# Linear attention and token/channel mixing: the first eight head pairs projected in float32, their numerators formed with tokens on partitions

## The chip, the cores and the metric

One core of one Trainium2 chip runs the kernel. The metric is the device time of one launch, in microseconds, as the median of several runs. TensorE (PE) multiplies matrices, VectorE (DVE), ScalarE (ACT) and GpSimd (POOL) work elementwise, SyncE (SP) issues DMAs. PEld is the loading of PE's stationary operand.

## What is computed

Per batch and head a feature map makes 256 positive features of each 64-wide query and key, a linear attention follows, and its output goes through a token mixer and a channel mixer. Shapes: batch 8, heads 8, sequence 576, head width 64, 128 features before the sign pair, token width 256, channel width 1536.

```python
def phi(x):
    proj = np.einsum('bhsd,df->bhsf', x, w_phi)
    proj = proj - np.max(np.abs(proj), axis=-1, keepdims=True)
    return np.concatenate([np.exp(proj), np.exp(-proj)], axis=-1)
q_p, k_p = (phi(q), phi(k))
kv = np.einsum('bhsf,bhsd->bhfd', k_p, v)
z = np.sum(k_p, axis=2)
num = np.einsum('bhsf,bhfd->bhsd', q_p, kv)
den = np.einsum('bhsf,bhf->bhs', q_p, z)[..., None] + 1e-06
out = num / den
...
xt = x.transpose(0, 2, 1)
h = np.maximum(xt @ w_tok1, 0.0) @ w_tok2
u = x + h.transpose(0, 2, 1)
return u + np.maximum(u @ w_ch1, 0.0) @ w_ch2
```

## The kernel before

Heads go in pairs: 4 pairs a batch, 32 in all. Nearly all matrix products are split in two float32r parts: a value is a high part plus a low part, and `mm3` (L77) makes three products of them (high by high, high by low, low by high). The weights of the mixers arrive as 64-bit numbers, and `convert` (L116) makes each block into its two parts: ACT takes an absolute value (L131), DVE does four steps on the bits (L132 to L135), ACT writes the high part and POOL the low part. 24 blocks of the channel weights and 7 of the token weights are made so, all in the first part of the program.

A pair passes these steps:

- **Projection** (`less_max`, L191). Pairs 0 to 3 (`i < PLAIN`) multiply 64-row slices of the loaded float32 tiles, queries on partitions 0 to 63 and keys on 64 to 127, by `wp` (L216); a float32 matmul is two PE records in the trace. Later pairs are first stacked by `stack` (L178): the high part on 64 partitions by DVE, the low part on the other 64 by POOL; then one float32r matmul of 256 columns gives both products (L212), ACT copies the second one out of PSUM (L219) and DVE adds (L221). DVE takes the largest absolute value (L226). The subtraction is on DVE for keys of pairs 0 to 3, on ACT for their queries, with a negated maximum from DVE (L230, L232), and on POOL for all later pairs (L234).
- **Keys** (`keys`, `add_kv`): ACT makes the two exponentials `kp` (L278), PE sums them into `pkv` (L300), 65 columns a matmul, the last column being the sum z. `kv` is copied out with z spread over 64 columns (L311), for later pairs as a high and a low part (L313).
- **Queries** (`queries`, `turn`, `numerators`): PE turns the projections so that features lie on partitions (L356), ACT makes `qf`, two signs (L363); for later pairs DVE and POOL split it into `qh` and `ql`. PE multiplies `kv` as stationary operand by `qf` (L389, pairs 0 to 3) or by the parts (L81, `pn<-qh`, `pn<-ql`): the result `pn` has channels on partitions, 320 or 256 tokens wide, and the spread z gives the denominator in the other half of the partitions. ACT copies the numerators, ACT (pairs 0 to 7, `EARLY`) or DVE adds the epsilon, DVE takes the reciprocal of the whole [128, 320] or [128, 256] tile (L401), POOL multiplies.

`token_mix` (L417) turns the attention output back to tokens on partitions with PE transposes (L423, `px`), splits it on ACT and DVE (`xh`, `xl`) and multiplies; `channel_mix` works on 18 tiles of 256 tokens (`h`, `acc`). Four streams of work and the conversion of the weights are woven together by `weave` with shares and step costs written in the code, and the build's scheduler then sets the order of every engine. PE, DVE, ACT and POOL each take their instructions in that order. The PSUM tag `rest` has three banks, which `pt`, `pn` and others share.

## Time and profile before

| | us |
|---|---|
| median of 3 runs | 1182.57 |
| lowest, highest | 1180.76, 1182.67 |
| span of the profiled execution | 1183.6 |
| PE busy | 1137.6 |
| DVE busy | 867.1 |
| POOL busy | 587.1 |
| ACT busy | 531.5 |

The profile is of one execution. Busy PE time is a poor measure here, since matmuls overlap in the pipeline: a matmul of 256 columns shows a duration of 0.28 us, while such matmuls start 0.12 us apart. The number of PE records in a stretch tells more. The clock column gives the share of TensorE's full clock that was granted: 1.00 is the higher of its two levels (2.4 GHz), 0.5 the lower (1.2 GHz); before the first change on record, some 30 us into the span, it tells nothing.

### The profile page before, as it was taken

What the parts mean: (1) busy time and instruction counts of PE and PEld (TensorE: products, weight loads), DVE (VectorE), ACT (ScalarE), POOL (GpSimd) and SP (SyncE); (2) the same over time, 40 slices, a digit from 0 to 9 for tenths busy, and PEclk for the clock granted to TensorE, in tenths of its full rate; (3) what the DMA queues carried; (4) which work ended last, traced back from release to release, by engine and by line L of the source; (5) the groups of instructions that cost most, each with busy time, mean ns of one, the idle gap of its engine ahead of it and who ended that gap; (6) DMA issues with size and microseconds to landing.
All of it is one profiled execution on the core that took longest, in us unless ns stands there. A gap on an engine that the chain in (4) does not pass through costs nothing.

```text
span 1183.6 us, 24087 instructions
## 1 busy us (share of the span) xinstructions
PE 1137.6 (96%) x9032; PEld 1102.0 (93%) x9032; DVE 867.1 (73%) x1782; ACT 531.5 (45%) x1545; POOL 587.1 (50%) x734
## 2 busy tenths in 40 slices
PE   8789897899999999999999999999999999999998
PEld 7667887898999999999999999999999999999998
DVE  7977899986777888887878677684787978763111
ACT  5767565453444445444444443343353544431110
POOL 3344775854555566465555455473564655431000
PEclk9679898999999999999999999999999999999999
DMA  9541222111111111111111011110111110000000
GB/s 232 150 135 28 72 84 71 50 31 28 31 40 32 49 31 32 49 32 49 32 34 46 20 31 49 30 50 1 49 31 49 32 48 12 19 1 19 19 19 19
DMA packets 65300, 54.31 MB, mean 46 GB/s; under 512 B 44768, under 2 KB 56416, under 8 KB 65184
## 3 DMA queue, kind: packets, MB, share of 16 engines
q1 hardware_dynamic: 63824, 52.41, 15.4%
q8 instruction: 72, 1.18, 0.4%
q10 hardware_dynamic: 1360, 0.36, 0.2%
q14 instruction: 44, 0.36, 0.1%
HBM read 43.32 MB, written 9.44 MB: 45 GB/s over the span
## 4 chain that ended last, share of the span: by engine, by line
PE 78%; DVE 11%; ACT 4%; issue 3%; POOL 2%; DMA 2%; SPq 0%; DVEq 0%; POOLq 0%; ACTq 0%
PE h L81 23%; PE acc L81 23%; PE pkv L300 8%; PE pn L81 7%; PE ph L81 3%; PE pa L81 3%; PE pt L356 3%; PE ppq L212 2%; PE ppk L212 2%; DVE qh L74 2%; PE pn L389 1%; DVE den L401 1%; PE px L423 1%; DMA rawc<-in_wc 1%; DVE bitsc L132 1%
## 5 line engine op out<-in xcount | busy, mean ns | idle before, releaser
L81 PE MATMUL acc<-gh,wc 128*128 128x256 f32 x1728 | 345.1, 283 | 0.0
L81 PEld LDWEIGHTS acc<-gh,wc 128*128 128x128 f32 x1728 | 276.0, 188 | 0.2 <-ACT gh L489 0.2
L81 PE MATMUL h<-uh,wc_h 128*128 128x256 f32 x864 | 246.8, 286 | 4.3 <-ACT wc_h L72 2.2
L81 PE MATMUL h<-uh,wc_l 128*128 128x256 f32 x864 | 245.9, 285 | 0.8 <-POOL wc_l L75 0.8
L81 PE MATMUL h<-ul,wc_h 128*128 128x256 f32 x864 | 243.9, 282 | 0.3 <-POOL ul L470 0.3
L81 PE MATMUL acc<-gl,wc 128*128 128x256 f32 x864 | 242.0, 282 | 0.6 <-DVE gl L490 0.6
L278 ACT ACTIVATE kp<-pmk 128x256 f32<-128x256 f32 (+1 forms) x320 | 109.2, 389 | 171.1 <-POOL pmk L234 168.1
L300 PE MATMUL pkv<-v,kp 128*128 128x65 f32 (+1 forms) x1152 | 165.7, 278 | 6.8 <-ACT kp L278 3.3
L81 PEld LDWEIGHTS h<-uh,wc_h 128*128 128x128 f32 x864 | 163.7, 190 | 5.8 <-ACT wc_h L72 2.6
L300 PEld LDWEIGHTS pkv<-v,kp 128*128 128x128 f32 x1152 | 155.9, 200 | 12.6 <-ACT kp L278 5.4
L75 POOL TENSOR_TENSOR ql<-qf,qh 128x320 fp32r<-128x320 f32 (+1 forms) x112 | 103.4, 923 | 127.7 <-DVE qh L74 110.8
L81 PEld LDWEIGHTS h<-uh,wc_l 128*128 128x128 f32 x864 | 163.4, 189 | 1.1 <-POOL wc_l L75 1.1
L81 PEld LDWEIGHTS h<-ul,wc_h 128*128 128x128 f32 x864 | 163.8, 190 | 0.5 <-POOL ul L470 0.5
L81 PEld LDWEIGHTS acc<-gl,wc 128*128 128x128 f32 x864 | 162.5, 188 | 0.7 <-DVE gl L490 0.7
L490 DVE SCALAR_TENSOR_TENSOR gl<-h,gh 128x512 fp32r<-128x512 f32 x108 | 73.5, 680 | 89.2 <-ACT gh L489 88.7
L74 DVE CAST qh<-qf 128x320 fp32r<-128x320 f32 (+1 forms) x224 | 106.5, 489 | 34.6 <-ACT qf L363 29.1
L401 DVE RECIPROCAL den<-den 128x320 f32<-128x320 f32 x64 | 124.6, 1947 | 3.2 <-ACT den L397 2.2
L363 ACT ACTIVATE qf<-pt 128x320 f32<-128x320 f32 (+1 forms) x256 | 92.6, 412 | 71.2 <-PE pt L356 68.5
L81 PE MATMUL pn<-qh,kv 128*128 128x320 f32 (+1 forms) x448 | 118.8, 302 | 3.5 <-DVE qh L74 1.5
L489 ACT ACTIVATE gh<-h 128x512 fp32r<-128x512 f32 x108 | 64.9, 601 | 116.0 <-PE h L81 115.2
L402 POOL TENSOR_TENSOR xt<-xt,den 128x320 f32<-128x320 f32 x64 | 53.7, 839 | 114.7 <-DVE den L401 87.8
L470 POOL TENSOR_TENSOR ul<-xt,uh 128x64 fp32r<-128x64 f32 (+3 forms) x120 | 62.2, 543 | 84.2 <-ACT uh L469 83.3
(110 smaller groups left out, 2415.3 us busy)
## 6 DMA issues: line engine op xcount, KB each, us to landing
raw<-in_qk SPq DMA_DIRECT2D x27, 576.0 KB, 3.7
rawc<-in_wc SPq DMA_DIRECT2D x24, 512.0 KB, 4.2
v<-in_vm SPq DMA_DIRECT2D x31, 256.0 KB, 3.3
out_x<-xt SPq DMA_DIRECT2D x12, 256.0 KB, 2.2
out_x<-xt SPq DMA_DIRECT2D x16, 192.0 KB, 2.0
raw<-in_w SPq DMA_DIRECT2D x8, 256.0 KB, 4.6
...
```

The source lines that it names most:

```text
L74: eng_hi.tensor_copy(hi, raw)
L75: eng_lo.tensor_tensor(lo, raw, hi.bitcast(F32), op=ALU.subtract)
L81: nc.tensor.matmul(o, a, m, start=first and i == 0, stop=last and i == 2, skip_group_check=group_ok)
L212: nc.tensor.matmul(ps[:, i].rearrange("p two f -> p (two f)"), t[:, c:c + P], wp2.rearrange("p two f -> p (two f)"), start=True, stop=True)
L278: nc.scalar.activation(kp[:, :len(us), sg], pm[:, :len(us)], AF.Exp, scale=1.0 - 2.0 * sg)
L300: nc.tensor.matmul(o, kp[:, n, sg], v, start=g == 0 and n == 0 and sg == 0, stop=u is None, skip_group_check=True)
L363: nc.scalar.activation(full, src, AF.Exp, scale=1.0 - 2.0 * sg)
L401: nc.vector.reciprocal(den, den)
L402: nc.gpsimd.tensor_tensor(x, x, den, op=ALU.mult)
L470: nc.gpsimd.tensor_tensor(l[:, d:d + n], t[:, c, o:o + n], h[:, d:d + n].bitcast(F32), op=ALU.subtract)
L489: nc.scalar.activation(gh, ph, AF.Relu)
L490: nc.vector.scalar_tensor_tensor(gl, ph, 0.0, gh.bitcast(F32), op0=ALU.max, op1=ALU.subtract)
```

## The change

Pairs 4 to 7 join pairs 0 to 3 (`PLAIN` 4 to 8): they are loaded by four DMAs a pair instead of one block for a pair of rows, aren't stacked, and are projected by float32 matmuls of 64 rows from the loaded tiles. In all eight pairs the subtraction of the maximum is one DVE instruction for queries too; the negated maximum and ACT's part in it are gone.

The numerators of pairs 0 to 7 (`ROWS`) are formed the other way round: a block of 128 (or 64) tokens of `qf` is the stationary operand, and `kv` with its sum column, 65 columns wide, moves. The result `pr` has tokens on partitions; both heads of a piece share a bank. DVE adds the epsilon to the few denominators, takes their reciprocals and multiplies into `rows`; one piece later (`flip`) PE turns `rows` to channels (`pf`) and ACT copies it to `xt`. The token mixer of batches 0 and 1 reads `rows` itself, without `px`, and makes `xl` on POOL.

Counted in the two orders: on PE 32 float32 `pn` matmuls, 96 float32r `pn` matmuls, 72 stacked projections and 40 `px` transposes go; 160 `pr` matmuls (32 of them with 64 tokens), 72 more float32 projections and 40 `pf` transposes come. DVE has 32 instructions fewer, ACT 148, POOL 73; SP has 12 more DMAs.

```diff
-PLAIN = 4
-EARLY = 8
+PLAIN = 8
+ROWS = 8
...
-        if base == 0:
-            nmx = column(wk, 2, tag="nmx", name=f"nmx{name}")
-            nc.vector.tensor_scalar(nmx[:, :n], mx[:, :n], -1.0, None, op0=ALU.mult)
-            for i in range(n):
-                nc.scalar.activation(pm[:, i], pr[:, i], AF.Identity, bias=nmx[:, i:i + 1])
-        else:
-            eng.tensor_tensor(pm[:, :n], pr, mx[:, :n].unsqueeze(2).to_broadcast([P, n, F]), op=ALU.subtract)
+        eng.tensor_tensor(pm[:, :n], pr, mx[:, :n].unsqueeze(2).to_broadcast([P, n, F]), op=ALU.subtract)
...
+        if i < ROWS:
+            kv = wk.tile([P, 2, 4, D], F32, tag="kv0", name=f"kv0_{i}", bufs=1)
+            kv = kv.rearrange("p s j d -> p (s j d)")[:, :4 * (D + 1)]
+            nc.scalar.copy(kv, pkv.rearrange("p s j d -> p (s j d)"))
+            kvs[i] = kv.rearrange("p (s j d) -> p s j d", s=2, j=2)
+            return
...
+            if row_major:
+                flip(*row_major)
+                yield 0.2
+            row_major = None
             if split_up:
                 yield from until(lambda: split_up[0] in kvs)
-                numerators(*split_up)
+                if split_up[0] < ROWS:
+                    row_major = row_numerators(*split_up)
+                else:
+                    numerators(*split_up)
                 yield 0.75
...
+    def row_numerators(i, k, j, qps):
+        b, p = divmod(i, NP)
+        h, p = divmod(p, 2)
+        n = 3 - k
+        if j == 0:
+            sums[0] = ps_w.tile([P, 2, 3, D + 1], F32, **REST, name=f"pr{i}_{k}")
+        pn = sums[0]
+        at = (D if j == 1 else 0) if k == 0 else 0
+        for u in range(n):
+            w, c = (P, at + u * P) if u < 2 else (D, 0 if j == 1 else 2 * P)
+            for sg in range(2):
+                nc.tensor.matmul(pn[:w, j, u], qps[sg][:, c:c + w], kvs[i][:, sg, j],
+                                 start=j == 0 and u == 0 and sg == 0, stop=j == 1 and u == n - 1 and sg == 1,
+                                 skip_group_check=True)
+        if j == 0:
+            return None
...
+        den = column(wk, 8, tag="dn", name=f"dn{i}_{k}")
+        for w, a, e in ((P, 0, 2), (D, 2, 3))[:2 - k]:
+            d = den[:w, 2 * a:2 * e].rearrange("p (j u) -> p j u", j=2)
+            nc.vector.tensor_scalar(d, pn[:w, :, a:e, D], 1e-6, None, op0=ALU.add)
+            nc.vector.reciprocal(d, d)
+            nc.vector.tensor_tensor(x[:w, :, a:e], pn[:w, :, a:e, :D],
+                                    d.unsqueeze(3).to_broadcast([w, 2, e - a, D]), op=ALU.mult)
+        return i, k
+
+    def flip(i, k):
+        b, p = divmod(i, NP)
+        make_xts(b)
+        x = rows_of[b, p // 2][:, 3 * k:3 * k + 3 - k, (p % 2) * P:(p % 2) * P + P]
+        pf = ps_w.tile([P, SEG[0][1]], F32, **REST, name=f"pf{i}_{k}")[:, :SEG[k][1]]
+        for u in range(3 - k):
+            w = P if u < 2 else D
+            nc.tensor.transpose(pf[:, u * P:u * P + w], x[:w, u], ident[:w, :w])
+        nc.scalar.copy(xts[b][k][:, p], pf)
+        if k == 1:
+            attended.add(i)
...
-            px = bank(b, [P, 2, P], f"px{b}_{h}_{u}", 1)
-            for c in range(2):
-                nc.tensor.transpose(px[:w, c], xt[k][:, 2 * h + c, o:o + w], ident)
+            if (b, h) in rows_of:
+                px = rows_of[b, h][:, u].rearrange("p (c d) -> p c d", c=2)
+            else:
...
-            split(xh, xl, px[:w], nc.scalar, nc.vector)
+            split(xh, xl, px[:w], nc.scalar, nc.gpsimd if (b, h) in rows_of else nc.vector)
```

The order of three places. First PE in the numerators of pair 0 (the last number but one of a name is not the pair; each tile has its own number). Before, with `pn` multiplied by 256 tokens at a time:

```order
L356 MATMUL pt_10_383<-ident,pmq_10_354 128x128 x2
L216 MATMUL ppq_00_449<-wp,pair_299 128x128 x2
L300 MATMUL pkv_359<-v_97,kp_2_380 128x65 x4
L300 MATMUL pkv_359<-v_97,kp_3_427 128x65 x4
L216 MATMUL ppq_01_487<-wp,pair_301 128x128
L216 MATMUL ppk_1_535<-wp,pair_497 128x128
L389 MATMUL pn_10_415<-qf_100_386,kv_0_320 128x256
L389 MATMUL pn_10_415<-qf_101_388,kv_0_320 128x256
L356 MATMUL pt_11_430<-ident,pmq_11_409 128x128 x2
```

After, from the end of the second piece of `pr`:

```order
L399 MATMUL pr_0_312<-kv_0_310,qf_010_323 64x65
L399 MATMUL pr_0_312<-kv_0_310,qf_011_325 64x65
L292 MATMUL pkv_344<-v_95,kp_2_370 128x65 x4
L214 MATMUL ppq_00_440<-wp,pair_289 128x128 x2
L214 MATMUL ppk_4_455<-wp,pair_291 128x128
L214 MATMUL ppq_01_476<-wp,pair_291 128x128 x2
L214 MATMUL ppk_0_492<-wp,pair_483 128x128 x2
L292 MATMUL pkv_344<-v_95,kp_3_420 128x65 x4
L423 MATMUL pf_0_403<-ident,rows_0_355 128x128 x2
L399 MATMUL pr_1_408<-kv_0_310,qf_100_376 128x65
```

The transposes `pf` stand 8 matmuls of the keys' sums and 7 projections behind the `pr` matmuls that they depend on, and the next `pr` stands behind them; before, nothing on PE at this place waits for a normalised numerator.

DVE at the same place, before, around the reciprocal of pair 0's first denominators:

```order
L132 TENSOR_SCALAR bitsc_1_1130<-bitsc_1_1130 128x512
L135 SCALAR_TENSOR_TENSOR bitsc_3_0_714<-rawc_3_0_712,bitsc_3_0_714 128x512
L134 SCALAR_TENSOR_TENSOR bitsc_0_870<-rawc_0_868,bitsc_0_870 128x512
L133 TENSOR_SCALAR bitsc_1_1130<-bitsc_1_1130 128x512
L401 RECIPROCAL den_0_325<-den_0_325 128x320
L226 TENSOR_REDUCE mxq_00_452<-ppq_00_449 128x2
L135 SCALAR_TENSOR_TENSOR bitsc_0_870<-rawc_0_868,bitsc_0_870 128x512
```

After, between the epsilon and the product of pair 0's first rows (`dn_0_356` is the denominators' tile, `rows_0_355` what `pf` turns):

```order
L133 SCALAR_TENSOR_TENSOR bitsc_2_0_537<-rawc_2_0_535,bitsc_2_0_537 128x512
L130 TENSOR_SCALAR bitsc_0_850<-bitsc_0_850 128x512
L226 TENSOR_TENSOR pmk_3_418<-ppk_3_413,mxk_3_416 128x256
L132 SCALAR_TENSOR_TENSOR bitsc_3_0_699<-rawc_3_0_697,bitsc_3_0_699 128x512
L411 RECIPROCAL dn_0_356<-dn_0_356 128x4
L224 TENSOR_REDUCE mxq_00_443<-ppq_00_440 128x2
L224 TENSOR_REDUCE mxk_4_457<-ppk_4_455 128x1
L131 TENSOR_SCALAR bitsc_0_850<-bitsc_0_850 128x512
L224 TENSOR_REDUCE mxq_01_479<-ppq_01_476 128x2
L130 TENSOR_SCALAR bitsc_1_1076<-bitsc_1_1076 128x512
L133 SCALAR_TENSOR_TENSOR bitsc_3_0_699<-rawc_3_0_697,bitsc_3_0_699 128x512
L412 TENSOR_TENSOR rows_0_355<-pr_0_312,dn_0_356 128x2x2x64
```

The one long reciprocal has become a reciprocal of 4 columns and a product; six conversion steps of the weights (`bitsc`) stand between the epsilon, which is the row ahead of these, and the product.

Second, DVE in the second batch. Before, queries of pair 4, the last keys of pair 5 and the stacking of the next pairs:

```order
L186 CAST stk_1660<-raw_1652 64x640
L75 TENSOR_TENSOR ql_010_1384<-qf_010_1381,qh_010_1383 128x320
L186 CAST stq_1680<-raw_1652 64x640
L221 TENSOR_TENSOR pq_11_1519<-ppq_11_1514,partq_11_1517 128x256
L221 TENSOR_TENSOR pk_4_1557<-ppk_4_1553,partk_4_1555 128x128
L74 CAST qh_100_1496<-qf_100_1494 128x256
L226 TENSOR_REDUCE mxq_11_1521<-pq_11_1519 128x2
L226 TENSOR_REDUCE mxk_4_1559<-pk_4_1557 128x1
L75 TENSOR_TENSOR ql_100_1497<-qf_100_1494,qh_100_1496 128x256
L449 SCALAR_TENSOR_TENSOR al_1_1420<-pa_1_1242,ah_1_1419 128x512
L74 CAST qh_101_1502<-qf_101_1500 128x256
L401 RECIPROCAL den_0_1327<-den_0_1327 128x320
```

After, where the same token mixer as in the rows before (the first batch's second half, `al_1`, `ph_1`) has come as far; `rows_0_1283` is of pair 4:

```order
L224 TENSOR_REDUCE mxk_4_1417<-ppk_4_1415 128x1
L226 TENSOR_TENSOR pmk_4_1419<-ppk_4_1415,mxk_4_1417 128x128
L410 TENSOR_SCALAR dn_0_1284<-pr_0_1203 128x4
L411 RECIPROCAL dn_0_1284<-dn_0_1284 128x4
L412 TENSOR_TENSOR rows_0_1283<-pr_0_1203,dn_0_1284 128x2x2x64
L410 TENSOR_SCALAR dn_0_1284<-pr_0_1203 64x2
L411 RECIPROCAL dn_0_1284<-dn_0_1284 64x2
L506 TENSOR_TENSOR xt_0_401<-ph_1_0_0_1338,xt_0_401 128x320
L412 TENSOR_TENSOR rows_0_1283<-pr_0_1203,dn_0_1284 64x128
L224 TENSOR_REDUCE mxk_0_1496<-ppk_0_1493 128x2
L224 TENSOR_REDUCE mxq_11_1349<-ppq_11_1346 128x2
```

The casts and differences of `qf`, the stacking and the long reciprocal are gone; denominators and rows stand there, and projections are read from PSUM directly.

Third, SP at the start. Before:

```order
L253 DMA pair_102<-in_qk 64x512
L253 DMA pair_104<-in_qk 64x640
L256 DMA pair_102<-in_qk 64x512
L256 DMA pair_104<-in_qk 64x640
L125 DMA raw_0_129<-in_w 128x256 x2
L125 DMA raw_3_173<-in_w 128x256 x2
```

After:

```order
L237 DMA raw_2536<-in_qk 64x1152
L245 DMA pair_100<-in_qk 64x512
L245 DMA pair_102<-in_qk 64x640
L248 DMA pair_100<-in_qk 64x512
L248 DMA pair_102<-in_qk 64x640
L123 DMA raw_0_125<-in_w 128x256 x2
```

The first block of `raw` (64 partitions of 1152 numbers: the keys of pair 4 before, of pair 8 now) stood nineteenth and is now the first transfer.

## Rows read from the trace of the kernel before

**Rows 1.** The page, its first two parts: busy time of the engines, then 40 equal slices of the span, DVE's busy tenths and TensorE's granted clock.

```profile
PE 1137.6 (96%) x9032; PEld 1102.0 (93%) x9032; DVE 867.1 (73%) x1782; ACT 531.5 (45%) x1545; POOL 587.1 (50%) x734
...
DVE  7977899986777888887878677684787978763111
...
PEclk9679898999999999999999999999999999999999
```

**Rows 2.** Busy time by stage: the stretch in us, its length, then for PE, PEld, DVE, ACT and POOL the busy time and the number of records, the granted clock, the DMA share and GB/s.

```profile
0.00:66.00 66.00, 54.21 (x238) 43.97 (x238) 58.20 (x122) 43.92 (x114) 22.58 (x33) 0.83 0.70 191
66.00:144.00 78.00, 71.64 (x409) 60.05 (x409) 59.78 (x121) 50.41 (x153) 39.61 (x42) 0.83 0.22 65
144.00:229.00 85.00, 72.74 (x543) 69.20 (x543) 82.51 (x143) 46.92 (x123) 60.34 (x62) 0.94 0.22 65
229.00:298.00 69.00, 67.13 (x551) 65.37 (x550) 51.53 (x108) 32.44 (x97) 37.52 (x48) 1.00 0.15 42
298.00:1183.00 885.00, 871.92 (x7300) 863.46 (x7298) 615.07 (x1293) 357.78 (x1061) 427.03 (x551) 1.00 0.11 32
```

**Rows 3.** What DVE waited for from 66 to 144 us, longest first: total us, times, longest.

```profile
DVE mxq L226 <- PE ppq L216: 10.0, 4, 3.2
```

**Rows 4.** The same for DVE from 144 to 229 us.

```profile
DVE pk L221 <- ACT xt L395: 1.6, 1, 1.6
```

**Rows 5.** What PE waited for from 144 to 229 us, the longest.

```profile
PE pt L356 <- POOL pmq L234: 2.3, 1, 2.3
PE h L81 <- ACT wc_h L72: 2.2, 1, 2.2
PE pkv L300 <- ACT bitsc L131: 1.8, 1, 1.8
```

**Rows 6.** PE in order of time near 240 us, full clock: start, duration, what.

```profile
240.28 0.28 PE L81 MATMUL h<-uh,wc_l 128*128 128x256 f32 x1
240.40 1.89 PE L300 MATMUL pkv<-v,kp 128*128 128x65 f32 x16
242.10 0.36 PE L81 MATMUL h<-uh,wc_h 128*128 128x256 f32 x1
```

**Rows 7.** PE in order of time from 92 to 108 us, full clock: float32 projections and numerators, and what started next.

```profile
92.60 1.16 PE L216 MATMUL ppq<-wp,pair 64*128 64x128 f32 x8
93.69 0.70 PE L389 MATMUL pn<-qf,kv 128*128 128x256 f32 x2
94.22 0.38 PE L356 MATMUL pt<-ident,pmq 128*128 128x128 f32 x2
...
98.57 0.71 PE L216 MATMUL ppq<-wp,pair 64*128 64x128 f32 x4
99.20 0.50 PE L212 MATMUL ppk<-wp,stk 128*128 128x256 f32 x2
...
101.31 0.70 PE L389 MATMUL pn<-qf,kv 128*128 128x320 f32 x2
101.94 0.71 PE L216 MATMUL ppq<-wp,pair 64*128 64x128 f32 x4
```

**Rows 8.** PE in order of time near 21 us: float32 projections of keys (`ppk`, partitions 64 to 127) alone and then in turn with those of queries (`ppq`, partitions 0 to 63).

```profile
20.55 1.01 PE L216 MATMUL ppk<-wp,pair 64*128 64x128 f32 x3
21.14 0.58 PE L216 MATMUL ppq<-wp,pair 64*128 64x128 f32 x1
...
21.95 0.42 PE L216 MATMUL ppq<-wp,pair 64*128 64x128 f32 x1
```

**Rows 9.** Groups of DVE instructions over the span, forms apart: count, busy us, mean ns of one, idle before.

```profile
L401 DVE RECIPROCAL den<-den 128x320 f32<-128x320 f32 x32 | 68.7, 2147 | 2.3 <-ACT den L397 1.9
L74 DVE CAST qh<-qf 128x256 fp32r<-128x256 f32 x112 | 60.6, 559 | 17.2 <-ACT qf L363 13.4 <-PE pn L81 2.8
L401 DVE RECIPROCAL den<-den 128x256 f32<-128x256 f32 x32 | 55.9, 1747 | 0.9 <-ACT den L397 0.3
...
L74 DVE CAST qh<-qf 128x320 fp32r<-128x320 f32 x112 | 45.8, 420 | 17.4 <-ACT qf L363 15.7
...
L75 DVE TENSOR_TENSOR ql<-qf,qh 128x320 fp32r<-128x320 f32 x56 | 37.6, 672 | 0.1
...
L313 DVE TENSOR_TENSOR kv<-pkv,kv 128x256 fp32r<-128x256 f32 x56 | 21.0, 416 | 12.4 <-ACT kv L311 12.3
...
L186 DVE CAST stk<-raw 64x640 fp32r<-64x640 f32 x28 | 16.5, 588 | 6.5 <-PE ppk L212 5.5
...
L234 DVE TENSOR_TENSOR pmk<-ppk,mxk 128x256 f32<-128x256 f32 x16 | 6.6, 412 | 0.2
...
L230 DVE TENSOR_SCALAR nmxt<-mxt 128x1 f32<-128x1 f32 x4 | 0.6, 140 | 0.0
```

**Rows 10.** The third of DVE's four conversion steps: count, shortest, median and longest ns, first and last start.

```profile
L134 DVE SCALAR_TENSOR_TENSOR bitsc<-rawc,bitsc x24: 627/692/1812, 29.6 to 216.6; 128x512 uint32<-128x512 uint32 x24
```

**Rows 11.** A group of POOL instructions over the span: a difference of two SBUF tiles of 256 columns.

```profile
L470 POOL TENSOR_TENSOR ul<-xt,uh 128x256 fp32r<-128x256 f32 x24 | 17.9, 765 | 60.7 <-ACT uh L469 60.5
```

**Rows 12.** A group of ACT instructions over the span.

```profile
L232 ACT ACTIVATE pmq<-ppq,nmxq 128x128 f32<-128x128 f32 x32 | 10.1, 366 | 4.7 <-DVE nmxt L230 3.0 <-DVE nmxq L230 1.5
```

**Rows 13.** DMA issues of SP in order of time: the first two, and later the first block of `raw`.

```profile
0.74 1.21 SPq L253 DMA_DIRECT2D pair<-in_qk  x2
...
17.29 0.59 SPq L245 DMA_DIRECT2D raw<-in_qk  x1
```

More of the change, by code (lines that the diff above doesn't have):

```diff
@@ L303, in add_kv @@
             return
+        if i < ROWS:
[4 more added lines that the diff above has]
+            return
         both = []
-        for k in range(1 if i < PLAIN else 2):
-            kv = wk.tile([P, 2, 4, D], F32 if i < PLAIN else F32R, tag=f"kv{k}", name=f"kv{k}_{i}", bufs=1)
+        for k in range(2):
+            kv = wk.tile([P, 2, 4, D], F32R, tag=f"kv{k}", name=f"kv{k}_{i}", bufs=1)
             for at, src in ((slice(0, 4, 3), pkv[:, :, :, :D]),
@@ L342, in queries @@
                     asked.add(i)
[L343 removed]
+                    tail = less_max(ts, [None], f"t{i}", plain, i < NP)
                     yield 0.11
[L345 removed]
+                pm = less_max(ts, [(j, 2 * k), (j, 2 * k + 1)], f"q{i}_{k}{j}", plain, i < NP)
                 turned = (i, k, j, pm, tail)
@@ L371, in turn, with make_xts @@
         return i, k, j, qps
-    dens, xts = {}, {}
-    def numerators(i, k, j, qps):
-        b, p = divmod(i, NP)
+    dens, xts, rows_of, sums = {}, {}, {}, {}
+    def make_xts(b):
         if b not in xts:
@@ L379, in numerators @@
                       wk.tile([P, NC_, SEG[1][1]], F32, tag="xt1", name=f"xt1_{b}", bufs=3)]
+    def row_numerators(i, k, j, qps):
[14 more added lines that the diff above has]
+            return None
+        if (b, h) not in rows_of:
+            rows_of[b, h] = wk.tile([P, 5, 2 * P], F32, tag="rows", name=f"rows{b}_{h}")
+        x = rows_of[b, h][:, 3 * k:3 * k + n, p * P:p * P + P].rearrange("p u (j d) -> p j u d", j=2)
+        den = column(wk, 8, tag="dn", name=f"dn{i}_{k}")
[17 more added lines that the diff above has]
+            attended.add(i)
+    def numerators(i, k, j, qps):
+        b, p = divmod(i, NP)
+        make_xts(b)
         x = xts[b][k][:, p]
@@ L387, in numerators @@
             w_hl = [kv[:, sg, 2 * j:2 * j + 2].rearrange("p z d -> p (z d)") for kv in kvs[i]]
-            if i < PLAIN:
-                nc.tensor.matmul(pn, w_hl[0], qps[sg], start=sg == 0, stop=sg == 1)
-            else:
-                mm3(pn, w_hl, qps[sg], sg == 0, sg == 1)
+            mm3(pn, w_hl, qps[sg], sg == 0, sg == 1)
         rows, drows = slice(j * D, j * D + D), slice(D - j * D, P - j * D)
@@ L537, in token_stream @@
             for h in range(2):
-                yield from until(lambda: b * NP + 2 * h + 1 in attended and (b > 0 or PLAIN - 1 in kvs))
+                yield from until(lambda: b * NP + 2 * h + 1 in attended and (b > 0 or NP - 1 in kvs))
                 yield from token_mix(b, h, xts[b])
```

28 lines of the change are left out of this document (12 added, 16 removed).

## The prediction

> **What bounds the kernel now.** I read the page first, then the stages, then who waits for whom in each. Over the span PE is busy 96% of the time, which alone says nothing [rows 1]. The stages tell more [rows 2]. From 298 us to the end PE runs 7300 records in 885 us, one per 0.121 us, at full clock, though DVE is busy for only 615 us of it: this stretch is bound by PE. Take 0.121 us as the pace of a saturated PE. Then the earlier stages lose the following: 0 to 66 us (stage A) has 238 records, worth 28.8 us, and loses 37.2; 66 to 144 (B) has 409, worth 49.6, and loses 28.4; 144 to 229 (C) has 543, worth 65.8, and loses 19.2; 229 to 298 has 551, worth 66.8, and loses 2.2. What the change can give lies in the 85 us lost in A to C, and pairs 0 to 7, which it touches, run there.
>
> Why is the time lost? In C, DVE is busy for 82.5 of 85 us [rows 2], and its longest wait is 1.6 us [rows 4]; PE waits for products of DVE, POOL and ACT, a few us in all [rows 5]. C is bound by DVE. In B, DVE is busy for 59.8 of 78 us and itself waits 10.0 us for query projections [rows 3]; the granted clock is 0.83 there, and PE is busy for 71.6 us [rows 2]. About 0.17 times 72, or 12 us, of B's loss is the lower clock, and 16 us are waits. In A, DVE is busy for 58.2 us of 66: DVE and the start.
>
> **The change, part by part. PE.** All prices are at full clock. 16 records of 65 columns take 1.70 us from their first start to the next instruction's [rows 6], so 0.213 us a matmul of two records, and 128 `pr` matmuls with 128 tokens cost 27.2 us. The 32 with 64 tokens aren't shown; by the same row they cost at most 0.21, and half of it if the 64 columns of weights count: I take 0.16, 5.1 us (3.5 to 6.8). Removed are 16 pairs of float32 `pn`: 0.63 us for one of 320 columns, 0.53 for one of 256 [rows 7], 18.6 us. Removed are 96 float32r `pn`: 256 columns start 0.12 us apart [rows 6], 320 by their columns 0.15, together 13.0 us. 72 stacked projections at 0.12 are 8.6 us. 72 float32 ones come: four took 1.09 us, and two took 0.63 twice [rows 7], so 0.27 to 0.32, I take 0.29: 20.9 us. 40 `pf` replace 40 `px`, the same transposes: nothing. Sum: 27.2 + 5.1 - 18.6 - 13.0 + 20.9 - 8.6 = 13 us more PE work (10 to 18), almost all in pairs 4 to 7, where float32r numerators and stacked projections were cheaper.
>
> **DVE.** Per pair of 4 to 7 go [rows 9]: 8 casts of `qf` (4 x 0.56 + 4 x 0.42 = 3.9), four differences `ql` (2.7), two long reciprocals (2.15 + 1.75 = 3.9), four stacking casts (about 0.59 each, 2.4), two differences of `kv` (0.8), two of `xl`, priced like these (0.8): 14.5 us. The sums `pq`, `pk` become subtractions of equal size. New are three epsilons and three short reciprocals, not in the trace: I price them like the smallest DVE instruction shown, 0.14 (`nmxt`), 0.8 us in all, at most 0.42 each if they stall as `nmxq`-sized work can, 2.5; and three products read from PSUM, at most 0.41 each (`pmk`), 1.2. Net 12.5 us less a pair (10.8 at the worst), 50 us in all. Pairs 0 to 3 lose reciprocals, `xl` and negated maxima (about 6) and gain the subtraction of queries (five instructions, 1.9) and the 2.0 above: 2 us less a pair.
>
> **ACT and POOL** lose about 150 and 70 instructions, among them the 32 subtractions of 0.37 us [rows 12]; neither is the bound (46.9 and 60.3 us of 85 in C [rows 2]), so I cost this at nothing; DVE covers it today, PE after. The new `xl` on POOL take about 0.77 us [rows 11] instead of DVE's 0.42, hidden as long as the next block's matmuls are behind others.
>
> **SP.** The block that now goes first takes about 0.6 us to issue [rows 13] ahead of pair 0's tiles, and it shares their DMA: 0.6 to 2 us in A, I take 1.5. The other 12 issues come when SP is idle: nothing.
>
> **The sum by stage.** A: DVE's first pairs get the queries' subtractions before the first reciprocals are saved, so no gain, +1.5 us (0 to +5). C: about half of the work of pairs 4 to 7 lies here, so 25 of DVE's 82.5 us go and leave 57; PE needs 65.8 plus half of the 13, 72. PE becomes the bound, as from 229 us on, where 2.2 of 69 us are lost. The clock of 0.94 need not rise at once: C's loss goes from 19 to 5, -14 (-18 to -8). B: DVE falls by some 15 us and stops being late; PE has 56 us of work in 78. I let most of the waits and a few us of the clock go: 28 to 15, -13 (-22 to -3). With +13 for PE: 1.5 - 14 - 13 + 13 = -12.5. From 298 us on nothing changes. The profiled span of 1183.6 becomes 1171; it lies 1.0 us above the median of 1182.6, so the time is **1170 us**, the case's own range 1161 to 1179.
>
> **A rule weighed.** Near 21 us three records of key projections took 0.20 us each alone, then seven records, keys and queries in turn, started 0.135 us apart [rows 8]. This is on partitions 64 to 127 and 0 to 63. The Trainium skill, TensorEngine Tiling (Array Packing), section Overview, says that products of at most 64 rows can run as two independent tiles, up to twice as fast; the trace agrees in part. A case of its own: had the projections of pairs 4 to 7 stood in turn, they would cost 0.135/0.20 of 20.9 us, 14.1, and the time would be **1163**. In the order, keys and queries of these pairs mostly stand apart, so it gets little chance.
>
> **The rivals.**
> *More* (1156): with DVE early, the clock stays at its higher level from 70 us on, and B and C run near PE's pace: B 28 to 6, C 19 to 2, -39, +1.5, and PE at its low bound of +10. For it: clock and DVE's lateness go together in B. Against: work there is still a few chains.
> *Nothing gained* (1183): the weights, not the pairs, hold C. Each block passes ACT, four DVE steps, ACT and POOL through single buffers, and PE waited for one (`wc_h`, 2.2 us [rows 5]). Then B and C lose only 7 less each: -14 + 1.5 + 13. For it: a conversion step has a median of 0.69 us and reached 1.81 [rows 10], and POOL gets new work. The Trainium skill, SBUF — State Buffer, section Who interferes with whom, says that a DVE instruction with two SBUF inputs and a GpSimd one that reads SBUF lock each other out for a whole instruction; this speaks against `xl` on POOL. By it the eight of the first batch could hold DVE by up to 6 us in B, 1176; but far more such POOL work leaves in pairs 4 to 7.
> *Slower* (1194): PE stands at the transposes `pf`. Before, no PE instruction near a pair waited for its normalised numerators; now 16 groups do, with the next `pr` behind them in PE's queue. Between epsilon and product of pair 0, six conversion steps and five other instructions stand on DVE, about 5.5 us at 0.4 to 0.7 each; between `pr` and `pf` PE has 15 matmuls, some 3.7 us at full clock, twice that at the lower one. If each of 16 groups waits 1.5 us, 24 us are lost: 1170 + 24. It decides wherever DVE's stretch is longer than PE's. Against: in pairs 4 to 7 DVE's rows stand close together, as its order shows.
>
> **How the numbers follow.** Chances: forecast 0.45, overlap 0.05, more 0.15, nothing gained 0.15, slower 0.20. The likeliest is 1170. The range, 1155 to 1190, takes in the first four and the lower third of the slower case. About 0.2%, 2.4 us, is what a measurement of this kernel can tell from no change. Faster: nearly all of the forecast (0.43), 0.05, 0.15, and a third of nothing gained (0.05), 0.68; same 0.07; slower 0.25.
>
> **What would show it.** Right: from 144 to 229 us DVE's busy share falls to about two thirds and PE's records come at 0.125 us or less; the saturated pace starts some 25 us earlier, and there are 13 us more of PE work in front of the same tail. `pr` at 0.21 us a matmul; the three small DVE steps together under 1.2 us. Wrong: waits of PE at `pf` for `rows` of over 10 us in all (slower); a stage B still at a clock near 0.8 and 78 us long; DVE still over 90% busy in C with conversions (nothing gained).

## The result, and the profile after

The changed kernel takes **1197.06 us** (1186.38 to 1199.03, 4 runs) against 1181.92 for the kernel before on the same chip: ratio 1.0106, 95% interval 1.0078 to 1.0135. It is 1.1% slower; 1170 was forecast, and 1155 to 1190 as range. One of the four executions took 1186.4 us, and its mean granted clock was 0.996; the profiled one, 1199.0 us with a span of 1197.2, had 0.988.

The page of the changed kernel, against [rows 1]: busy time, then DVE's busy tenths and TensorE's granted clock in 40 slices.

```profile
PE 1169.0 (98%) x9264; PEld 1135.3 (95%) x9264; DVE 805.1 (67%) x1750; ACT 488.3 (41%) x1397; POOL 520.1 (43%) x661
...
DVE  7972458744867779787878677585786878763111
...
PEclk9995999999999999999999999999999999999999
```

DVE lost 62 us of work, and the slices show where: 2 to 5 tenths from 90 to 180 us, where it had 7 to 9. PE is busy 31 us longer. Busy time by stage, against [rows 2], columns as there:

```profile
0.00:66.00 66.00, 55.69 (x250) 49.24 (x251) 56.94 (x129) 34.29 (x79) 23.11 (x30) 1.00 0.71 196
66.00:144.00 78.00, 77.45 (x448) 70.00 (x446) 34.42 (x97) 27.80 (x80) 11.03 (x13) 0.82 0.18 50
144.00:229.00 85.00, 82.25 (x624) 73.99 (x623) 61.62 (x133) 40.35 (x100) 25.28 (x26) 1.00 0.26 75
229.00:298.00 69.00, 68.65 (x551) 65.46 (x551) 29.87 (x78) 21.96 (x63) 24.61 (x31) 1.00 0.12 38
298.00:1183.00 885.00, 874.67 (x7313) 866.50 (x7312) 619.86 (x1312) 363.25 (x1075) 436.09 (x563) 1.00 0.11 32
```

From 66 us on PE hardly stands (0.6 us in B, 2.8 in C), yet its records come at 78/448 = 0.174 us in B and 85/624 = 0.136 us in C; the saturated pace of the tail is 0.121, as before. So PE is the bound and is slow. The tail has the same work and nearly the same pace. The start of the keys and values of pair 8, a step that every version has, moves from 240 to 251 us, and that of pair 9 from 265 to 281. The last 7264 PE records, the same but for 8 in both kernels, start at 302 us before and at 318 now, 16 us later; at the end 13.6 are left. So all is lost ahead of some 318 us.

One stretch of the same profile shows why B is slow, in the columns of the stages:

```profile
92.00:117.50 25.50, 25.50 (x110) 23.18 (x110) 6.01 (x18) 5.72 (x16) 0.50 (x1) 0.50 0.09 23
```

PE is busy for all of it, and the granted clock is at its lower level. By the trace's clock events it was up only from 86.7 to 90.2 us before it rose for good at 117.5. (Ahead of the first event the column says 1.00; the spacing of the records, 0.213 us where it is 0.112 later, tells the lower level.) The kernel before had it up at 30.4 to 37.2, 57.7 to 64.5, 78.2 to 85.0, and from 91.8 us with few gaps.

What PE waited for from 0 to 300 us, and DVE from 66 to 229 (total us, times, longest), against [rows 3 to 5] (rows left out are marked):

```profile
PE ppk L214 <- DMA pair<-in_qk: 6.3, 2, 5.9
PE pt L361 <- ACT xt L424: 3.5, 1, 3.5
...
PE pf L423 <- DVE dn L410: 0.2, 1, 0.2
```
```profile
DVE mxk L224 <- PE ppk L214: 13.9, 9, 5.1
DVE mxq L224 <- PE ppq L214: 13.9, 11, 2.7
DVE dn L410 <- PE pr L399: 10.0, 7, 2.5
...
```

Now DVE waits for PE. At `pf` PE waited 0.2 us in all. DVE's new small steps, from its groups over the span (count, busy us, mean ns of one, idle before):

```profile
L411 DVE RECIPROCAL dn<-dn 128x4 f32<-128x4 f32 x16 | 2.8, 173 | 0.3
L410 DVE TENSOR_SCALAR dn<-pr 128x4 f32<-128x4 f32 x16 | 2.5, 157 | 11.6 <-PE pr L399 11.6
...
L411 DVE RECIPROCAL dn<-dn 64x2 f32<-64x2 f32 x8 | 1.2, 150 | 0.1
L410 DVE TENSOR_SCALAR dn<-pr 64x2 f32<-64x2 f32 x8 | 1.1, 141 | 0.0
```

### The profile page after: what moved, and what is told of

Read it like the earlier page. It is cut to its first block, busy times and chain, and to the rows that moved or that the text cites. A ratio compares the mean times of both kernels' runs of the same rounds, so it can differ in the third digit from the quotient of the medians.

```text
span 1197.2 us, 24261 instructions
## 1 busy us (share of the span) xinstructions
PE 1169.0 (98%) x9264; PEld 1135.3 (95%) x9264; DVE 805.1 (67%) x1750; ACT 488.3 (41%) x1397; POOL 520.1 (43%) x661
## 3 DMA queue, kind: packets, MB, share of 16 engines
q1 hardware_dynamic: 64528, 52.41, 15.2%
## 4 chain that ended last, share of the span: by engine, by line
PE 81%; DVE 9%; ACT 2%; POOL 2%; issue 2%; DMA 2%; SPq 0%; DVEq 0%; POOLq 0%; ACTq 0%
PE h L81 22%; PE acc L81 22%; PE pkv L292 10%; PE pn L81 5%; PE ph L81 4%; PE pa L81 3%; PE pt L361 3%; PE pr L399 3%; PE ppq L214 2%; PE ppk L214 2%; PE ppk L210 2%; PE ppq L210 2%; DVE qh L74 1%; DMA rawc<-in_wc 1%; DVE den L446 1%
## 5 line engine op out<-in xcount | busy, mean ns | idle before, releaser
L292 PE MATMUL pkv<-v,kp 128*128 128x65 f32 (+1 forms) x1152 | 172.7, 286 | 3.4 <-ACT kp L270 2.8
L292 PEld LDWEIGHTS pkv<-v,kp 128*128 128x128 f32 x1152 | 162.0, 208 | 8.4 <-ACT kp L270 3.9
L75 POOL TENSOR_TENSOR ql<-qf,qh 128x320 fp32r<-128x320 f32 (+1 forms) x96 | 88.9, 926 | 114.2 <-DVE qh L74 101.3
L74 DVE CAST qh<-qf 128x320 fp32r<-128x320 f32 (+1 forms) x192 | 87.1, 468 | 42.4 <-ACT qf L368 37.4
L81 PE MATMUL pn<-qh,kv 128*128 128x320 f32 (+1 forms) x384 | 99.7, 298 | 0.5 <-DVE al L497 0.3
L446 DVE RECIPROCAL den<-den 128x320 f32<-128x320 f32 (+1 forms) x48 | 93.5, 1949 | 0.9
L185 POOL TENSOR_TENSOR stq<-raw,stq 64x512 fp32r<-64x512 f32 (+1 forms) x48 | 69.6, 1450 | 44.1 <-DVE stq L184 37.4
```

The lines of the kernel that those rows point to most:

```text
L74: eng_hi.tensor_copy(hi, raw)
L75: eng_lo.tensor_tensor(lo, raw, hi.bitcast(F32), op=ALU.subtract)
L81: nc.tensor.matmul(o, a, m, start=first and i == 0, stop=last and i == 2, skip_group_check=group_ok)
L185: nc.gpsimd.tensor_tensor(t[lo:lo + D], src, t[base:base + D].bitcast(F32), op=ALU.subtract)
L292: nc.tensor.matmul(o, kp[:, n, sg], v, start=g == 0 and n == 0 and sg == 0, stop=u is None, skip_group_check=True)
L446: nc.vector.reciprocal(den, den)
```

## The experiments

The table gives the median time, the ratio to the kernel before with its interval, and from the clock events of the profiled execution how many of the first 120 us TensorE was at 1.2 GHz (the time ahead of the first event counts as such) and when it last rose in them. Ratio and interval are worked out from all executions, so a ratio can differ a little from the quotient of two medians.

The last column is of one execution, and executions of one kernel differ. The profiled ones of e9 and e13 are among the shortest of theirs (1184.6 and 1182.9), that of e1 is the longest (1192.6), and that of the kernel before has a mean granted clock of 0.975, where 53 of the 71 taken beside the experiments have 0.980 or more. The nine of e10 run from 1174.3 us at a mean clock of 0.978 to 1186.5 at 0.965: by 0.013 of 1178 us, twice since the lower level is half the clock, some 30 us more at 1.2 GHz, and 12 us longer. The ten of e1 run from 1182.0 at 0.989 to 1192.6 at 0.976, again some 30 us more at the lower level and 11 longer. So without any edit a us at 1.2 GHz comes with 0.3 to 0.4 us of time, an estimate from these two kernels; the mean counts the time ahead of the first clock event as full, so only kernels in which that comes early (e10 at 11 us, e1 at 34) tell it.

Most edits also change the order in which the scheduler puts PE's work, among the first pairs and far behind them. From the 2000th to the 8500th PE record the changed kernel and e7, in one order, take 785.5 us in both; e3, e8 and e9, in a second, 790.2 to 790.5; e12 and e15, in a third, 793.9 and 794.5. The instructions are nearly the same ones, and within each group the starts lie 9 to 25 us apart. So the tail's time goes with its order to within 1 us here, and up to 9 us of a difference between two kernels can come from there.

| kernel | us | ratio | us at 1.2 GHz, last rise |
|---|---|---|---|
| before | 1182 | 1 | 71, 92 |
| changed | 1197.1 | 1.0106 [1.0078, 1.0135] | 114, 117.5 |
| e1 old numerators, pairs 0-3 | 1185.1 | 1.0024 [0.9998, 1.0051] | 81, 92 |
| e2 stacked projections, pairs 4-7 | 1182.5 | 1.0001 [0.9964, 1.0038] | 94, 94 |
| e3 padded projections | 1174.5 | 0.9917 [0.9893, 0.9941] | 58, 92 |
| e4 before + numerators 0-3 | 1180.8 | 0.9981 [0.9961, 1.0002] | 88, 88 |
| e5 before, padded | 1175.5 | 0.9935 [0.9910, 0.9961] | 32, 100 |
| e6 padded in 4-7 only | 1182.3 | 0.9989 [0.9973, 1.0005] | 91, 91 |
| e7 full tails | 1208.0 | 1.0209 [1.0183, 1.0235] | 118, 118.5 |
| e8 padded, full tails | 1167.9 | 0.9862 [0.9824, 0.9901] | 52, 86 |
| e9 padded in 0-3 only | 1189.8 | 1.0056 [1.0036, 1.0075] | 51, 89 |
| e10 new numerators, stacked, padded | 1178.5 | 0.9973 [0.9950, 0.9996] | 62, 90 |
| e11 float32 projections padded, old numerators | 1159.5 | 0.9809 [0.9789, 0.9829] | 24, 72 |
| e12 wide new numerators | 1197.7 | 1.0135 [1.0110, 1.0160] | 62, 72 |
| e13 float32 projections, old numerators | 1190.2 | 1.0071 [1.0037, 1.0105] | 49, 87 |
| e14 e11 with an earlier load | 1158.2 | 0.9807 [0.9793, 0.9822] | 16, 71 |
| e15 e3 with wide numerators | 1173.0 | 0.9937 [0.9916, 0.9959] | 36, 74 |

Two theories stood at the start. **Clock**: with narrow work TensorE stays at 1.2 GHz for longer. **Price**: products on 64 rows cost more than I took, because PE pays on entering and leaving that form.

**e1.** Pairs 0 to 3 get the old float32 numerators back.

```diff
-ROWS = 8
+ROWS_FROM, ROWS = 4, 8
...
-        if i < ROWS:
+        if in_rows(i):
```

> The changed kernel with one part undone: the numerators of pairs 0 to 3 again with keys and values as the stationary operand (32 float32 matmuls of 256 or 320 columns in place of 80 with 65 columns). Theory clock (narrow numerators in the first batch keep TensorE's clock at its lower level until 117 us): the granted clock goes up near 90 us for good, as in the kernel before, and most of the loss goes: 1175 to 1187 us. Theory price (the loss is the dearer matmuls of pairs 4 to 7): pairs 4 to 7 are unchanged, so at most some 4 us better than the changed kernel: 1190 to 1197 us.

Measured: 1185.1 us, 12 less than the changed kernel, with pairs 4 to 7 untouched. The stretch of 92 to 117.5 us in e1:

```profile
92.00:117.50 25.50, 25.40 (x186) 21.58 (x185) 18.72 (x39) 18.12 (x52) 3.19 (x4) 1.00 0.17 46
```

186 records in place of 110, at the higher level. The profile is of the longest of e1's ten executions; eight of the others have a higher mean clock, 0.984 to 0.989 in place of 0.976. Theory clock holds, in the clock and in the time: the edit is in pairs 0 to 3 alone, most of them ahead of this stretch.

**e2.** Projections of pairs 4 to 7 stacked again.

```diff
-PLAIN = 8
+PLAIN = 4
```

> The changed kernel with the other part undone: projections of pairs 4 to 7 again from stacked operands, 128 rows, one float32r matmul of 128 columns for each unit, as in the kernel before; the numerators stay with tokens on partitions for all eight pairs. Theory price (the 72 float32 projections with 64 rows cost about 0.4 us each with the change of form, not 0.29): TensorE loses some 20 to 25 us of work in pairs 4 to 7, DVE gets its stacking casts back; 1175 to 1183 us. Theory clock: the clock still goes up only near 117 us, and with it the loss stays: 1188 to 1197 us.

Measured: 1182.5 us, 14.6 less, as theory price said; but the clock too rises earlier, at 94 us. The new numerators for all eight pairs, with the old projections, are thus worth nothing either way against the kernel before.

**e3.** Same matmuls, no 64-row form: the weights are padded with 64 rows of zeros, and the whole loaded tile is read.

```diff
-                nc.tensor.matmul(ps[:, i, 0], t[rows, c:c + P], wp[rows], start=True, stop=True)
+                nc.tensor.matmul(ps[:, i, 0], t[:, c:c + P], wpz[base], start=True, stop=True)
```

> The changed kernel, but the float32 projections read all 128 rows of the loaded tile against weights that are zero in the other 64 rows, so the same number of matmuls and columns without a 64-row form. Adds two fills of GpSimd and two small loads at the start. Theory price by change of form: entering and leaving the 64-row form costs about 0.2 us each time, and it goes for 144 projections: 10 to 25 us faster than the changed kernel, 1172 to 1187 us, with the projections of a pair 0.11 us a record after a numerator. If the projections' price is only that of float32 (two records), the time stays within 3 us of the changed kernel. Theory clock alone: within 4 us of the changed kernel, clock up near 117 us still.

Measured: 1174.5 us, 22.5 less, and faster than the kernel before. The same place of the program at full clock, PE in order of time, in the changed kernel and then in e3 (start, duration, what):

```profile
155.73 0.50 PE L399 MATMUL pr<-kv,qf 128*128 128x65 f32 x3
156.16 0.71 PE L214 MATMUL ppk<-wp,pair 64*128 64x128 f32 x4
156.80 0.44 PE L361 MATMUL pt<-ident,pmq 128*128 128x128 f32 x2
```
```profile
133.98 0.61 PE L408 MATMUL pr<-kv,qf 128*128 128x65 f32 x4
134.43 0.66 PE L223 MATMUL ppk<-wpz,pair 128*128 128x128 f32 x4
134.93 0.38 PE L370 MATMUL pt<-ident,pmq 128*128 128x128 f32 x2
```

Read starts, not durations: two projections take 156.80 - 156.16 = 0.64 us on 64 rows, 0.50 on 128. And the three `pr` records ahead take 0.43, 0.143 each, where four take 0.45, 0.112 each, in e3: about 0.1 us is paid ahead of the run as well. Inside the run a record takes 0.112 in both, so it is a price of the change, about 0.24 us a run, not of the matmul. The Trainium skill, TensorEngine Tiling (Array Packing), section Tiling Modes, Key Properties, says it: "Changing tiling mode (not just tile) drains the TensorE". The trace agrees, with this 0.24 us; I had cited another sentence of that page and missed this one.

**e4.** The kernel before with the new numerators in pairs 0 to 3 alone.

```diff
-PLAIN = 8
-ROWS = 8
+PLAIN = 4
+ROWS_FROM, ROWS = 0, 4
```

> The kernel before with one part of the change alone: numerators with tokens on partitions for pairs 0 to 3 (pairs 4 to 7 as before, the query subtraction of pairs 0 to 3 on ACT as before). Theory clock: the clock stays low until some 110 us instead of 92, and the time is over that of the kernel before by 6 to 12 us: 1188 to 1194 us. Theory price: 80 narrow numerators replace 32 wide float32 ones at no more than 1 to 4 us of TensorE work, so 1181 to 1186 us.

Measured: 1180.8 us, the same as before within its interval, though the clock stands at 1.2 GHz for 88 us and not 71. There the lower clock cost nothing that shows, which speaks against clock as the whole story.

**e5.** The kernel before with e3's edit for its own 72 projections.

> The kernel before, with nothing of the change, but the 72 float32 projections of pairs 0 to 3 read all 128 rows against zero-padded weights. Theory price by change of form: the kernel before paid the same price for its own 72 projections, half of what the changed kernel pays, so 5 to 12 us come off: 1170 to 1177 us, and the change by itself, freed of the price, is worth about nothing (1174.5 against this). Rival, price hidden in the start: pairs 0 to 3 wait for loads and for DVE anyway, so within 3 us of the kernel before, 1179 to 1183 us, and then the change is worth some 7 us once the price is gone.

Measured: 1175.5 us, 6.7 less. The kernel before paid the price too; the whole change with padding (e3) is worth 1.0 us against it, less than the spread of either.

**e6 and e9.** e3's edit in pairs 4 to 7, and in pairs 0 to 3.

```diff
+                if int(name[1:].split("_")[0]) >= 4:
+                    nc.tensor.matmul(ps[:, i, 0], t[:, c:c + P], wpz[base], start=True, stop=True)
```

> The changed kernel with the projections padded to 128 rows in pairs 4 to 7 alone; those of pairs 0 to 3 stay in the 64-row form. Theory price by change of form at full clock in pairs 4 to 7: more than half of the 22 us of the kernel padded throughout come back, since TensorE is busy without a gap there: 1180 to 1185 us. Theory clock (the 64-row form of the first batch is what holds the clock low until 117 us): the clock still goes up near 115 us and less than a third comes back: 1190 to 1196 us.

> The changed kernel with the projections padded to 128 rows in pairs 0 to 3 alone; pairs 4 to 7 keep the 64-row form. Theory clock (while 64-row products run, the clock stays low; with 128 rows it rises from 10 us on): the clock shows its higher level in parts of the first 60 us, falls while pairs 4 to 7 are projected with 64 rows, and goes up for good near 110 us; together with the price of the change of form that is no longer paid in some 25 runs of projections (0.135 us before, 0.16 in, 0.135 behind each at the lower clock, 11 us), 10 to 16 us come off: 1181 to 1187 us. Theory price alone: no more than 11 us come off, and the clock's history is that of the changed kernel.

Measured: 14.7 and 7.3 us less than the changed kernel, together 22.0, close to what e3 gives at once; some of that is chance, since e3 and e9 share a tail that takes 5 us more than the changed kernel's. Both missed a part: e6's clock rises at 91 us, not at 115, and e9's goes up at 89 us and stays up to 280, while pairs 4 to 7 are still on 64 rows. From 92 to 117.5 us, e6 and then e9:

```profile
92.00:117.50 25.50, 25.48 (x209) 23.74 (x208) 12.24 (x37) 12.06 (x34) 2.92 (x4) 1.00 0.18 48
```
```profile
92.00:117.50 25.50, 25.50 (x203) 23.17 (x203) 13.93 (x41) 11.68 (x35) 3.13 (x5) 1.00 0.14 36
```

So the 64-row form of pairs 4 to 7 does not by itself hold the clock down: e9 runs them at the higher level there, the changed kernel runs the same kind of work at the lower one.

e9 and e3 isolate the price. Their PE orders are the same at all but 14 of 9264 places, and both run at the higher level from 92.4 to 273.3 us; what differs is the form of the projections in pairs 4 to 7. From 144 to 229 us, e3 and then e9:

```profile
144.00:229.00 85.00, 80.58 (x674) 77.86 (x673) 61.56 (x128) 38.71 (x98) 34.14 (x34) 1.00 0.25 72
```
```profile
144.00:229.00 85.00, 82.06 (x629) 75.52 (x629) 60.94 (x127) 36.01 (x88) 32.95 (x32) 1.00 0.24 72
```

At PE's 600th record e9 is 3.0 us ahead (109.6 against 112.6), at the 2000th 7.6 behind (298.3 against 290.7), with one dip of the clock of 6.8 us in each: 10.6 us in the 44 runs of 64-row products that lie between, 0.24 a run. The two profiles are 7.9 us apart, the medians 15.2.

**e7 and e8.** The 64-token tails in the full form, on the changed kernel and on e3.

```diff
-            w, c = (P, at + u * P) if u < 2 else (D, 0 if j == 1 else 2 * P)
+            w, c = P, at + u * P if u < 2 else 0 if j == 1 else 2 * P
...
-            nc.tensor.transpose(pf[:, u * P:u * P + w], x[:w, u], ident[:w, :w])
+            nc.tensor.transpose(pf[:, u * P:u * P + P], x[:, u], ident)
```

> The changed kernel, projections as they are, but the numerators and transposes of the 64-token tails in the full 128-row, 128-column form (the last block's first half is then computed over and not used); DVE handles a group in one set of three steps, not two. Theory price by change of form: 32 numerator matmuls with 64 columns of weights and 16 transposes of 64 rows also pay some 0.1 to 0.2 us on entering and on leaving, about 40 pieces: 3 to 8 us come off, 1189 to 1194 us. Rival, only the 64-row projections pay: the longer tails cost up to 2 us more: 1196 to 1199 us.

> The changed kernel with both: projections padded to 128 rows and tails in the full form, so that no product of the first eight pairs has a 64-row or 64-column form. Theory price by change of form: below the kernel with padded projections alone by 2 to 6 us, 1168 to 1173 us, 0.8 to 1.2% faster than the kernel before. Rival: as the kernel with padded projections, 1173 to 1177 us.

Measured: 1208.0 us, 11 more, a miss for both theories; and 1167.9, 6.6 less than e3, as forecast. In e7 the order of the work comes out otherwise: from 40 to 70 us PE waited

```profile
PE ppk L218 <- issue: 2.0, 1, 2.0
PE ppk L218 <- DVE pmk L230: 1.6, 1, 1.6
PE pf L428 <- DVE rows L418: 1.6, 1, 1.6
PE ppt L218 <- DVE pmq L230: 1.6, 1, 1.6
```

6.8 us, 2.7 more than the 4.1 of the changed kernel there. That is a quarter of the 11; the rest stays open.

**e10 and e11.** Each half of the change freed of the 64-row form: the numerators alone (stacked projections in pairs 4 to 7, PLAIN = 4), and the float32 projections alone (old numerators, float32, in all eight pairs).

```diff
-            mm3(pn, w_hl, qps[sg], sg == 0, sg == 1)
+            if i < PLAIN:
+                nc.tensor.matmul(pn, w_hl[0], qps[sg], start=sg == 0, stop=sg == 1)
+            else:
+                mm3(pn, w_hl, qps[sg], sg == 0, sg == 1)
```

> The change's numerators alone, freed of the 64-row form: numerators with tokens on partitions for all eight pairs, projections of pairs 4 to 7 stacked as before, those of pairs 0 to 3 padded to 128 rows. Against the kernel before with padded projections (1175.5): theory numerators pay (DVE relieved, no float32r splits of the queries' exponentials): 1168 to 1173 us. Rival, the numerators are worth nothing: 1174 to 1178 us.

> The change's projections alone, freed of the 64-row form: float32 projections padded to 128 rows for all eight pairs, numerators in the old layout (keys and values stationary, 256 or 320 columns, float32, for all eight pairs). Removed from the changed kernel with padded projections: 320 narrow matmuls of two records (68 us at the higher clock's 0.213); added: 64 wide float32 ones at 0.53 to 0.63 (37 us), and DVE's long reciprocals. If TensorE sets the end: 20 us or more faster than 1174.5, 1150 to 1158 us, so the narrow numerators lose. If DVE sets it in the first 230 us: 1170 to 1182 us.

Measured against e5 (1175.5): the numerators alone 1178.5, 3 more, well within the spread of e10's executions (1174.3 to 1186.5); the projections alone **1159.5**, 16 better. The new numerators are the part that loses: from e11 to e3 they cost 15 us. Their price on PE is not the reason. e11 at full clock, PE in order of time:

```profile
124.89 1.24 PE L451 MATMUL pn<-qf,kv 128*128 128x320 f32 x4
125.96 0.27 PE L372 MATMUL pt<-ident,pmq 128*128 128x128 f32 x1
...
129.73 1.03 PE L451 MATMUL pn<-qf,kv 128*128 128x256 f32 x4
130.59 0.27 PE L372 MATMUL pt<-ident,pmq 128*128 128x128 f32 x1
```

1.07 and 0.86 us for two matmuls, so 32 x 0.54 + 32 x 0.43 = 31 us for all; 160 narrow ones at 0.21 to 0.22 are about 32 to 35. The clock differs. The stretch of 66 to 92 us, e3 and then e11:

```profile
66.00:92.00 26.00, 23.72 (x106) 21.89 (x106) 20.05 (x35) 11.38 (x29) 14.98 (x11) 0.50 0.47 151
```
```profile
66.00:92.00 26.00, 22.17 (x141) 19.28 (x142) 23.96 (x45) 19.68 (x53) 8.98 (x8) 0.93 0.47 137
```

In the first 120 us e11 is at 1.2 GHz for 24 us, e3 for 58. The 34 us between them are worth up to 17 us of full-clock work. Of the 16 us between the two profiles, 11 have arisen where the last 7264 records start (280 and 291 us), and 4.5 come behind, in e3's order of the tail. That the 11 come from the clock is argued here; e15 tries it.

**e12 and e15.** Numerators with zeros beside them, so that each matmul runs over 130 columns, on the changed kernel and on e3. The edit neither adds nor removes a 64-row projection.

```diff
-                nc.tensor.matmul(pn[:w, j, u], qps[sg][:, c:c + w], kvs[i][:, sg, j],
+                nc.tensor.matmul(pn[:w, :, u], qps[sg][:, c:c + w], kvs[i][:, sg, j],
```

> The changed kernel with each numerator matmul against a zero-padded operand of 130 columns (both heads, the other head's half zero and added to its sum), the 64-row projections unchanged. Theory narrow numerators hold the clock low: the clock goes up by 95 us and 5 to 10 us come off in spite of somewhat longer matmuls, 1187 to 1194 us. Theory 64-row form holds it low: up at 115 us or later still, and the longer matmuls add 2 to 8 us: 1199 to 1206 us.

> The changed kernel with padded projections and with each numerator matmul against a zero-padded operand of 130 columns (both heads). Theory the narrow numerators lose by the clock: the time at the lower clock in the first 92 us falls from 65 to 40 us or less, worth 12 us, against 160 matmuls of two records that grow by some 0.03 us a record at the higher clock, 10 us: 1168 to 1176 us. Rival, they lose by their own price and the clock follows something else: the clock's history stays that of the padded kernel and the longer matmuls add 8 to 12 us: 1182 to 1188 us.

Measured: in e12 the clock rises at 72 us and stays up to 208, where the changed kernel has it up from 117.5, and the time at 1.2 GHz falls from 114 to 62 us (e15: 58 to 36). From 66 to 92 us, the changed kernel (at 1.2 GHz up to 86.7, ahead of its first clock event) and then e12:

```profile
66.00:92.00 26.00, 25.45 (x128) 22.97 (x127) 14.92 (x39) 9.73 (x27) 6.73 (x7) 0.96 0.34 103
```
```profile
66.00:92.00 26.00, 24.48 (x171) 21.32 (x170) 13.83 (x37) 12.34 (x35) 7.18 (x7) 0.89 0.32 96
```

171 records in place of 128. So the clock rose earlier with wider numerators, though the order changed with them: the first 2000 records of e12 agree with those of the changed kernel in 54% of their places. Yet the times hardly move: 1197.7, where 5 to 10 us less was expected, and 1173.0, in its range. The gain is there at first: PE's 2000th record starts at 307 us in e12 and at 318 in the changed kernel, though twelve `pr` records that took 1.31 us now take 1.57. Then it is given back: the 8500th starts at 1101 and at 1103. The clock is not why, at 1.00 in both from 320 to 600 us. The order of the tail is the likeliest reason: in e12's these 6500 records take 794 us, in the changed kernel's 785.5. No run changes the order alone.

e15 shows the same. At the 2000th record it is 9 us ahead of e3 (282 and 291), and its tail, in e12's order, gives 4 of them back. Where the last 7264 records start it is only 2 us behind e11 (282 and 280). So ahead of the tail nearly all of what the narrow numerators lost to e11 is gone with wider ones, though these take no less of PE's time: theory clock holds there, with the reserve that e15's order differs from e3's too.

**e13.** The changed kernel without its numerators (e11 with the 64-row form).

> The changed kernel without its numerators: float32 projections in the 64-row form for all eight pairs, numerators in the old layout (wide, float32). Theory numerators lose by the clock in any setting: 10 to 18 us off the changed kernel, 1179 to 1187 us, clock up for good by 95 us with brief rises before. Rival, the 64-row form alone holds the clock low and the numerators lose nothing here: 1192 to 1198 us.

Measured: 1190.2 us, 6.9 less than the changed kernel, but this median lies between two groups: four executions took 1182.0 to 1187.2, as in the first forecast, and four 1193.1 to 1195.6, in the second. The profile is of the first group (1182.9), with the clock up earlier (49 us at 1.2 GHz), as the first theory has it; the second group has no trace, so the two theories stay undecided here. Against e11 the 64-row form costs 23 to 36 us here.

**e14.** e11 with the padded weights loaded ahead of the stacked ones.

> The fastest kernel so far (float32 projections padded to 128 rows, numerators in the old layout, 1159.5) with the padded weights loaded before the stacked ones, which are needed only from pair 8 on. Theory the start is bound by these loads: TensorE's first projection comes 1 to 3 us sooner and the time falls by as much, 1156 to 1159 us. Rival, the pair's tiles come later than the weights anyway: within 1 us, 1158.5 to 1160.5 us.

Measured: 1158.2 us, 1.2 less than e11 and inside the first forecast; PE's first projection starts at 7.15 us (6.82 in e11), after a wait for the pair's tiles, so its reason failed. e11 and e14 beat both kernels, the one before by 1.9%.

## Why the prediction was wrong

**What held.** PE, not DVE, bounds C. DVE lost 62 us of work, about 58 forecast; its busy share from 144 to 229 us is 61.6/85, 72%. The four small steps take 0.62 us together in a group of three blocks, under the 1.2 I asked for. The tail has the same work and takes 2.7 us less. The rival *slower* named 1194, near the result, by a mechanism that is not there: PE waited 0.2 us at `pf`. *Overlap* was right as a mechanism, where keys and queries stood in turn; too few do. PE in order of time in the changed kernel, the first and the last of such a run and what came next:

```profile
120.93 0.37 PE L214 MATMUL ppq<-wp,pair 64*128 64x128 f32 x1
120.94 0.37 PE L214 MATMUL ppk<-wp,pair 64*128 64x128 f32 x1
...
121.38 0.27 PE L214 MATMUL ppk<-wp,pair 64*128 64x128 f32 x1
121.58 0.55 PE L292 MATMUL pkv<-v,kp 128*128 128x65 f32 x3
```

Eight records took 0.65 us; in e3's form they would take 8 x 0.112 = 0.9. *More* asked for a clock that stays up from 70 us (its sum gives 1155, not 1156). e11 and e14, which have it, are the fastest; e12 has it too, from 72 us, and gains nothing over the changed kernel.

**Step 1 that failed: B, "28 to 15, -13".** I let DVE's waits and some of the lower clock go. The waits went: PE's idle time fell from 6.4 to 0.6 us in B and from 12.3 to 2.8 in C. But in B there were only these 6.4, by the busy time in [rows 2]; my 16 us of waits were what was left of 28 after the clock's 12. And the clock, which was to give a few us back, took more: B has 48 us at 1.2 GHz where it had 26, worth some 24 us of full-clock work in place of 13, and the first 120 us have 114 in place of 71. I had read in [rows 2] that clock and DVE's lateness go together in B, and took the second for the cause. It isn't: with DVE early and PE busy for 25.5 of 25.5 us the clock stayed down, and edits to the numerators, with the order that came with them, moved its rise: wide ones in pairs 0 to 3 to 92 us, in a kernel 12 us faster (e1), narrow ones with zeros beside them to 72, 11 us ahead at the 2000th record (e12).

**Step 2: the projections at 0.29 us.** [Rows 7] gave it from starts of the run alone; what the change of form costs ahead of it (0.1 us) lay in the matmul before, and so also in the 0.63 that I took for a numerator of 320 columns, 0.54 in e11. Short runs of two or four records, the usual ones in pairs 4 to 7, pay 0.24 us each. The changed kernel has 47 runs that start after 117.5 us, so 11 us in all, for which the sum had no term. In C the changed kernel runs 624 records and e3 674 in the same 85 us: 50 x 0.121 = 6 us there.

**Step 3: the sum for numerators, 27.2 + 5.1 - 18.6 - 13.0.** As a sum of PE work it held to a few us: 32 to 35 us came, and the float32 ones that went cost 15.4 by e11's prices, not 18.6. That the numerators cost up to 15 us (e11 to e3) was missing. Of the 11 us ahead of the tail, widening them takes 9 back (e15), so the clock, for which the sum had no term, is the likeliest reason, though no run has it apart from the order; the rest is the order of the tail. With stacked projections they cost 0 to 3 (e2, e10).

Of e3's 22.5 us, the price in pairs 4 to 7 is some 11 (e9 against e3). How the rest divides between clock, price ahead of 117 us and order stays open: no run of the padded form changes one of them without the others.
